# Sign words on GpSimd, dummy transposes at the start, and two new tables of places in an attention and two-layer kernel

## The chip, the cores and the metric

One core of one Trainium2 chip. The metric is the device time of one execution in microseconds; the kernel before takes 914.72 us (median of three runs, 914.27 to 915.67).

## The reference

Three stages follow each other. Attention with rotated q and k, four batches of eight heads, 576 positions, 64 columns a head; then a gated layer on 2304 tokens; then a second layer with a softmax-weighted activation and a normalisation.

```python
q_rot, k_rot = (rotate(q), rotate(k))
scores = scale * np.matmul(q_rot, k_rot.transpose(0, 1, 3, 2))
attn = np.exp(scores - np.max(scores, axis=-1, keepdims=True))
attn = attn / (np.sum(attn, axis=-1, keepdims=True) + 1e-09)
x = np.matmul(attn, v)                       # then laid out as 2304 x 512
gate = 1.0 / (1.0 + np.exp(-(x @ w_gate)))   # 512 x 1536
x = gate * (x @ w_val) @ w_out               # 1536 x 512
h = x @ w_in                                 # 512 x 1024
solu = h * softmax(h)
ln = (solu - mean) / np.sqrt(var + 1e-06) * g_ln
out = ln @ w_out2                            # 1024 x 512
```

The weights of the layers come as 64-bit floats. The kernel reads them as pairs of 32-bit words and makes 32-bit floats of them itself.

## The kernel before, in words

**Two-term products.** Every 32-bit operand is split into a high part, as the matmul takes it, and a low part (the rest): ScalarE or VectorE copies the high part, VectorE or GpSimd subtracts. A product is three matmuls (high x high, high x low, low x high) or, in attention, stacked so that two do.

**Attention** works on 16 pairs of heads, nine tiles a pair (four for each head and one for the 64 left positions of both). For each pair q and k are loaded and rotated on GpSimd (lines 162 and 170; the first pair is rotated mostly on VectorE, lines 186 and 170), transposed on TensorE (the banks, lines 222 and 225), split into stacks (370 and 373; for pair 0 lines 249, 251 and 256), and some blocks are copied by DMA (line 238). A tile is then: scores on TensorE (291), row maximum on VectorE (298), exponential on ScalarE (303), transposes of the result on TensorE (379), their split on ScalarE (370) and VectorE (373), and the products with v (420). Scores alternate between two PSUM buffers, so the scores of tile n+2 wait for the exponential of tile n. The results are added (431) and scaled (351) on GpSimd.

The order of all of that is not found while the kernel is built. Every job has a name such as `scores.4.0@0` (its tile, step and pair) and a number in the table NEED, to which 16.83 times the pair is added. `emit_attention` sorts the jobs by that number into one queue for each engine; each queue is then issued strictly in that order. The other figures of an attention job (its cost `took`, its gate, its port) are not read by it.

**The first pair** is prepared ahead of the table: loads, rotation, and the transposes of three banks (0 is k, 1 is q, 2 is the left positions of both). `stack_first(h, step, m)` then evacuates them for head h: step 0 the 512 main positions, step 1 the 64 left ones, with m 0 and 1 the high parts of k and q on ScalarE, m 2 and 3 the low parts on VectorE, and step 2 copies k's block to the other half. In the table these are `first.h.step.m`.

**The gated layer** runs three groups of weights s over three blocks of tokens b of 768 each. Each block has four units (two gates, two values) of 42 or 48 matmul rows on seven products of quarters, and two output halves. Weights are made ahead of their use by `decode`: a load of raw words; the magnitude on ScalarE (463); the sign word (466), an OR with the magnitude (469) and an OR with the low word (474) on VectorE. Then come sums (483) and splits (486, 494). `make_pair` does two decodes for each of four units from s=1 on, `make_plain` two in all, `make_unit` one for each of twelve output weights, `keep_p` eight and `keep_i` eight for the last stage: 46 decodes. Six more weights are decoded during attention by `job_early`, which calls the same three steps. Tokens are split into xs by `split_x` (535, 540, 544). In the output halves results leave PSUM on ScalarE or VectorE (486) and go to memory, from s=1 on by DMAs of GpSimd's queue that add (1457).

**The planner of these stages** is `run_jobs`. Each job has an engine or a choice of two, a cost, what it reads and writes, and a due time `need`. On each engine, of the jobs that are ready first, the one due first is taken; TensorE's own order is fixed. Jobs marked with a port are kept from running on VectorE and GpSimd together.

**The last stage** computes the hidden layer, the normalisation and the second product by tiles of 128 tokens in the same planner.

The lines the change and the prediction touch: `qk_bank` (212 to 228), `w_sign` (465), the block after `table` (651 to 671), `job_scores` (723), the NEED table (1027), `decode` (1204), `KEEP_I` (1316), and `run_jobs` (1721).

Of the kernel before, what the change touches and what calls it, by code (L numbers as in the profile page):

```python
# [20 lines left out]
def kernel(  # L21
# [21 lines left out]
    nc = tc.nc  # L43
# [605 lines left out]
    if True:  # L649
# [72 lines left out]

    def job_scores(g):
# [7 lines left out]
        took = (1.06 if order[n] is None else 0.53) * (2.0 if g < 4 else 1.0)  # L731
        writes = [one(f"S{g % 2}")] + ([one(f"sum{i % 4}", 0, NTL)] if n == 0 else [])
        ajob(nc.tensor, took, lambda: found.__setitem__(("s", g), scores(i, n)), reads, writes)
# [8 lines left out]
    def turned_out(took, fn, reads, hi_at, lo_at, cols):  # L742
        t, key = bank_t(), ("t", turns[0])
        ajob(nc.tensor, took, lambda: found.__setitem__(key, fn()), reads, (t,))
        ajob(A, 0.045 + cols / 1190, lambda: [evac_h(*ev) for ev in found[key]], (t,), hi_at)
        ajob(V, 0.07 + cols / 960, lambda: [evac_l(*ev) for ev in found.pop(key)], [t] + hi_at, lo_at)

    def job_te(i, n):
# [3 lines left out]
        turned_out(0.436 * (2.0 if i * NTL + n < 2 else 1.0), lambda: transpose_e(i, n), [one(f"e{(i * NTL + n) % 7}", 0, 1)], hi_at, lo_at, 512)  # L752

    def job_corner(i):
        hi_at, lo_at = ([one(f"etl{h}{a}", MAIN, S) for h in range(2)] for a in range(2))
        turned_out(0.03, lambda: transpose_corner(i), [one(f"e{(i * NTL + 4) % 7}", 1, 2)], hi_at, lo_at, 128)
# [10 lines left out]
    def job_attend(i, h, j, m0, m1):  # L767
# [4 lines left out]
        if m1 == 9:  # L772
            e = (A, V)[SLOTS["uw"][2 * h + j]]
            ajob(e, 0.365 if e is V else 0.3, lambda: high(e, *found["av"][0][1:]), (one("AV"),), (one(uw, *c),))
# [21 lines left out]
    def job_weigh_out(i):  # L796
        ajob(V, 0.2, lambda: weigh_out(i, 0), (found.pop(("tr", i)),), (one("rt"),))
# [35 lines left out]
    def job_split_v(i):  # L833
        raw, hi, lo = one(f"rawv{i % 2}", 0, 3), one(f"vs{i % 2}", 0, 1), one(f"vs{i % 2}", 1, 2)
        ajob(A, 0.63, lambda: split_v(i, 0), (raw,), (hi, lo, one("order_vs")))
# [124 lines left out]
    for m, t in enumerate((7.9, 10.0, 10.25)):  # L960
# [60 lines left out]
    for m in chunks:  # L1021
# [939 lines left out]
```

## Time and profile before

| what | value |
|---|---|
| median of three runs | 914.72 us |
| profiled execution, its own time | 915.11 us |
| its span, first to last instruction | 913.2 us |
| mean granted clock of TensorE | 0.997 |
| busy: TensorE, VectorE, ScalarE, GpSimd | 882.9, 810.2, 653.5, 339.3 us |

The span is what the rows below divide; 1.9 us of the execution's time lie outside it. Attention fills the span to about 290 us, the gated layer from there to about 705, the last stage the rest. TensorE's matmuls are pipelined, so a row's length is that of one matmul from its start to its last result, and the next begins before.

### The profile page before, as it was taken

The numbers are of one execution on the slowest core, as the hardware profiler recorded it, in microseconds if no ns is written. First come the engines' busy times: TensorE is split into PE (matmuls) and PEld (weight loads), VectorE is DVE, ScalarE is ACT, GpSimd is POOL, SyncE is SP. The second block draws the span as 40 slices with busy tenths as digits, with TensorE's granted clock in tenths as the row PEclk, the third lists the DMA queues.
The fourth block names the chain that finished last, engine by engine and source line by source line (L and its number), as shares of the span: only waits on it lengthen the run. The fifth ranks groups of instructions, "written<-read, shape, count | busy, mean of one in ns | idle before, by whom it ended". The sixth has DMA issues, their size and how long they took to land.

```text
span 913.2 us, 16106 instructions
## 1 busy us (share of the span) xinstructions
PE 882.9 (97%) x5354; PEld 833.1 (91%) x5354; DVE 810.2 (89%) x1523; ACT 653.5 (72%) x1379; POOL 339.3 (37%) x296
## 2 busy tenths in 40 slices
PE   4999999999999999999999999999999999999998
PEld 3999999999998999999999999999999877888886
DVE  5999999999997798999998999999987499999971
ACT  4999999999995465666667666666565276777751
POOL 7679899898845000011011121212030243233200
PEclk9999999999999999999999999999999999999999
DMA  4667777678663762425275864659599834454332
GB/s 127 159 183 196 205 200 197 184 209 214 155 165 112 221 216 81 151 81 196 86 230 135 260 133 145 129 174 229 179 250 364 185 124 93 99 109 81 81 70 46
DMA packets 120882, 147.33 MB, mean 161 GB/s; under 512 B 44752, under 2 KB 90080, under 8 KB 120800
## 3 DMA queue, kind: packets, MB, share of 16 engines
q1 hardware_dynamic: 113888, 136.87, 51.4%
q0 software_dynamic: 6912, 9.44, 7.1%
q8 instruction: 42, 0.69, 0.3%
q14 instruction: 40, 0.33, 0.1%
HBM read 77.76 MB, written 37.30 MB: 126 GB/s over the span
## 4 chain that ended last, share of the span: by engine, by line
PE 73%; DVE 19%; issue 3%; DMA 2%; ACT 2%; POOL 0%; SPq 0%; DVEq 0%; ACTq 0%
PE s L291 9%; PE av L420 8%; PE te L379 7%; DVE xs L544 2%; PE tq L222 2%; PE far_c L1869 2%; PE far_b L1869 2%; PE far_c L1871 2%; PE far_b L1870 2%; PE far_c L1870 2%; PE far_b L1871 2%; PE tk L400 1%; DVE w L469 1%; PE near_a L630 1%; PE near_a L629 1%
## 5 line engine op out<-in xcount | busy, mean ns | idle before, releaser
L298 DVE TENSOR_REDUCE nm<-s 128x1 f32<-128x576 f32 x144 | 108.2, 752 | 11.5 <-PE s L291 9.0
L303 ACT ACTIVATE e<-s,nm 128x576 f32<-128x576 f32 x144 | 107.7, 748 | 7.4 <-DVE nm L298 6.0
L291 PE MATMUL s<-st 128*128 128x288 f32 x512 | 96.6, 312 | 5.5 <-DVE st L251 3.9
L373 DVE TENSOR_TENSOR et<-te,et 128x512 fp32r<-128x512 f32 x144 | 95.8, 676 | 1.4 <-ACT et L370 1.3
L420 PE MATMUL av<-et,vs 128*128 128x288 f32 x512 | 94.4, 312 | 0.4 <-POOL vs L202 0.4
L1457 POOL DMA_DIRECT2D yd<-yst x40 | 36.0, 1280 | 141.1 <-ACT yst L486 141.1
L370 ACT CAST et<-te 128x512 fp32r<-128x512 f32 x144 | 81.2, 587 | 7.8 <-PE te L379 6.4
L379 PE MATMUL te<-ident,e 128*128 128x128 f32 x576 | 81.9, 274 | 2.5 <-DVE et L373 2.4
L291 PEld LDWEIGHTS s<-st 128*128 128x128 f32 x512 | 75.1, 193 | 6.8 <-ACT st L249 4.2
L420 PEld LDWEIGHTS av<-et,vs 128*128 128x128 f32 x512 | 73.3, 191 | 0.7 <-POOL vs L202 0.6
L379 PEld LDWEIGHTS te<-ident,e 128*128 128x128 f32 x576 | 67.4, 141 | 5.1 <-DVE et L373 2.5
L540 ACT CAST xs<-xst 128x384 fp32r<-128x384 f32 x110 | 50.7, 518 | 13.7 <-DVE xst L535 11.5
L544 DVE TENSOR_TENSOR xs<-xst,xs 128x384 fp32r<-128x384 f32 x112 | 56.4, 548 | 2.2 <-ACT xs L540 2.0
L1538 POOL TENSOR_TENSOR xs<-xst,xs 128x512 fp32r<-128x512 f32 (+1 forms) x14 | 17.5, 1254 | 72.7 <-ACT xs L1535 72.7
L431 POOL TENSOR_TENSOR x_sb<-uw,um 64x576 f32<-64x576 f32 x30 | 43.2, 1439 | 2.5 <-DMA um<-uw 0.4
L494 POOL TENSOR_TENSOR wv<-w,wv 128x512 fp32r<-128x512 f32 (+1 forms) x3 | 5.2, 1743 | 103.3 <-ACT wv L486 103.3
L170 POOL TENSOR_TENSOR turned_t<-raw_t,other_t 128x576 f32<-128x576 f32 (+1 forms) x30 | 40.5, 1369 | 1.2
L463 ACT ACTIVATE mag<-raw_w 128x512 f32<-128x512 f32 x52 | 34.9, 676 | 7.9 <-DMA raw_w<-in_moe_w_val_dram 3.7
L162 POOL TENSOR_TENSOR other_t<-raw_t,rope_sb 128x1152 f32<-128x1152 f32 x14 | 37.4, 2674 | 5.6 <-DMA raw_t<-in_q_dram 4.5
L162 POOL TENSOR_TENSOR raw_t<-raw_t,rope_sb 128x1152 f32<-128x1152 f32 x14 | 37.3, 2664 | 1.1
L1811 POOL TENSOR_TENSOR st<-st,mhalf 128x1 f32<-128x1 f32 x18 | 15.9, 884 | 54.9 <-DVE st L1810 53.7
L629 PE MATMUL near_a<-xs,wg 128*128 128x384 f32 x96 | 32.3, 337 | 2.1 <-ACT held L1363 2.1
(475 smaller groups left out, 3068.4 us busy)
## 6 DMA issues: line engine op xcount, KB each, us to landing
st<-st SPq DMA_DIRECT2D x45, 288.0 KB, 4.0
xst<-xd SPq DMA_DIRECT2D x32, 384.0 KB, 6.0
raw_w<-in_moe_w_out_dram SPq DMA_DIRECT2D x20, 512.0 KB, 4.5
yd<-yst POOLq DMA_DIRECT2D x40, 192.0 KB, 6.5
st<-st SPq DMA_DIRECT2D x47, 144.0 KB, 2.4
raw_w<-in_moe_w_gate_dram SPq DMA_DIRECT2D x12, 512.0 KB, 4.3
raw_w<-in_moe_w_val_dram SPq DMA_DIRECT2D x12, 512.0 KB, 3.7
cd<-mag SPq DMA_DIRECT2D x22, 256.0 KB, 5.5
```

The lines of the kernel that those rows point to most:

```text
L162: eng.tensor_mul(out=(o, x)[step], in0=x, in1=w.to_broadcast([P, n, 2, D // 2]))
L291: nc.tensor.matmul(ps[:, j, :HALF], w, x, start=m == 0, stop=m == len(mm) - 1)
L298: nc.vector.tensor_reduce(out=nm, in_=ps[:, :, :HALF], axis=AX.XY, op=ALU.max, negate=True)
L303: nc.scalar.activation(out=e.rearrange("p (j c) -> p j c", j=2), in_=ps[:, :, :HALF], func=AF.Exp, bias=nm, accum_out=sums[i][:, n:n + 1],)
L370: nc.scalar.copy(out=h_out, in_=ps)
L373: nc.vector.tensor_sub(out=l_out, in0=ps, in1=h_out.bitcast(F32))
L379: nc.tensor.transpose(ps[:, r * P:(r + 1) * P], e[:, r * P:(r + 1) * P], ident)
L420: nc.tensor.matmul(av[:, :HALF], *mm[m], start=m == 0, stop=m == len(mm) - 1)
L431: eng.tensor_add(out=x_sb[hp][rows, b * S:(b + 1) * S], in0=uws.pop((i, h))[rows], in1=uws[i][rows])
L540: nc.scalar.copy(out=t[:, 0], in_=here)
L544: l_eng.tensor_sub(out=t[:, 1], in0=here, in1=t[:, 0].bitcast(F32))
L629: nc.tensor.matmul(out, wh, t[:, 0], start=fresh and j == 0, stop=False, skip_group_check=not fresh)
```

## The change

1. **Sign words.** `decode` no longer masks the sign on VectorE. GpSimd multiplies the upper raw word, taken as a float, by zero, which leaves a zero with that sign. `job_early` keeps the mask on VectorE.
2. **Dummies.** Transposes of the identity into a PSUM tile of the attention products that is not read: 30 before the three banks of pair 0, 16 behind them, and 5, 5 and 4 behind the scores of tiles 1, 2 and 3 of pair 0.
3. **Tables.** All but three of NEED's 446 numbers are new. A second table, SHIFT, with 945 entries, is added to the due times of the jobs of the later stages, which get names for that.
4. **Others.** `qk_bank` sets the stacks at every part, since part 2 may now be first; costs and gates of attention jobs are changed; the second layer's first weights are prepared 6 and 5 us earlier in their blocks.

```diff
     def qk_bank(i, part):
-        if part == 0:
-            stacks[i, 0] = st_t[i % 2][0]
-            stacks[i, 1] = st_t[i % 2][1]
+        stacks[i, 0], stacks[i, 1] = st_t[i % 2]
...
+    def w_zero(raw, dst):
+        nc.gpsimd.tensor_scalar(out=dst.bitcast(F32), in0=words(raw)[1].bitcast(F32), scalar1=0.0, scalar2=None, op0=ALU.mult)
...
+        idle_ps = ps_av.tile([P, 512], F32, tag="av", name="idle")
+
+        def keep_clock(n):
+            for _ in range(n):
+                nc.tensor.transpose(idle_ps[:, 0:P], ident, ident)
+
+        keep_clock(30)
         first.extend(qk_bank(0, part)[0][2] for part in range(3))
-        pass
+        keep_clock(16)
...
+    IDLE_AFTER = {1: 5, 2: 5, 3: 4}
...
-        took = (1.06 if order[n] is None else 0.53) * (2.0 if g < 4 else 1.0)
+        took = 1.06 if order[n] is None else 0.53
+        if i == 0 and n in IDLE_AFTER:
+            took += 0.11 * IDLE_AFTER[n]
...
+        def run():
+            found["s", g] = scores(i, n)
+            if i == 0 and n in IDLE_AFTER:
+                keep_clock(IDLE_AFTER[n])
...
     NEED = {
...
-        "early_split.1.0.1": 315.64, "early_split.1.1.0": 293.71, "early_split.1.1.1": 316.34, "first.0.0.0": -33.81,
-        "first.0.0.1": -62.21, "first.0.0.2": -32.31, "first.0.0.3": -12.85, "first.0.1.0": -47.13, "first.0.1.1": -19.51,
-        "first.0.1.2": -23.78, "first.0.1.3": -7.03, "first.0.2.0": -23.49, "first.0.2.1": -19.51, "first.1.0.0": -47.43,
-        "first.1.0.1": -21.09, "first.1.0.2": -39.4, "first.1.0.3": -6.96, "first.1.1.0": -21.89, "first.1.1.1": -14.81,
-        "first.1.1.2": -8.4, "first.1.1.3": -5.83, "first.1.2.0": -34.61, "first.1.2.1": 1.45, "join.0.0": 34.59,
...
+        "early_split.1.0.1": 329.84, "early_split.1.1.0": 307.9, "early_split.1.1.1": 321.54, "first.0.0.0": -155.18,
+        "first.0.0.1": -148.61, "first.0.0.2": -124.38, "first.0.0.3": -91.43, "first.0.1.0": -90.42, "first.0.1.1": -149.16,
+        "first.0.1.2": -100.02, "first.0.1.3": -104.32, "first.0.2.0": -67.98, "first.0.2.1": -41.76, "first.1.0.0": -71.56,
+        "first.1.0.1": -41.22, "first.1.0.2": -84.48, "first.1.0.3": -21.85, "first.1.1.0": -30.56, "first.1.1.1": -2.47,
+        "first.1.1.2": -66.08, "first.1.1.3": -14.93, "first.1.2.0": -101.44, "first.1.2.1": -74.49, "join.0.0": 35.91,
...
+    plain_job, names_of = job, []
+    SHIFT = {
+        "unit.1.2.0.17": -14, "unit.1.2.0.18": 0.8, "unit.1.2.0.3": -3.9, "unit.1.2.0.4": 17.4, "unit.1.2.0.8": -2.5,
...
+        "x.2.0.28": 14.4, "x.2.0.3": 7.5, "x.2.0.30": 12, "x.2.0.33": -4.9, "x.2.0.34": -0.6, "x.2.0.35": 5.4,
...
+    }
+    def place(*name):
+        step[:] = [".".join(map(str, name)), None, 0]
+
+    def job(eng, took, fn, reads=(), writes=(), need=0.0, port=None):
+        key = f"{step[0]}.{step[2]}"
+        step[2] += 1
+        names_of.append(key)
+        plain_job(eng, took, fn, reads, writes, need + SHIFT.get(key, 0.0), port)
...
     def decode(kind, n, dst, dst_at, need):
...
-        job(V, 0.34, lambda: w_sign(raw, dst), (r,), (dst_at,), need - 5, True)
+        job(G, 0.9, lambda: w_zero(raw, dst), (r,), (dst_at,), need - 5, False)
...
-    KEEP_I = {(2, 0): (0, 36.0), (2, 1): (1, 25.0)}
+    KEEP_I = {(2, 0): (0, 30.0), (2, 1): (1, 20.0)}
```

## Rows read from the trace of the kernel before

**Rows 1.** The page: busy time of each engine, and TensorE's granted clock in 40 slices.

```profile
PE 882.9 (97%) x5354; PEld 833.1 (91%) x5354; DVE 810.2 (89%) x1523; ACT 653.5 (72%) x1379; POOL 339.3 (37%) x296
PEclk9999999999999999999999999999999999999999
```

**Rows 2.** Stretches: length, then busy us (instructions) of each engine, granted clock, DMA.

```profile
100.00:150.00 50.00, 50.00 (x398) 48.02 (x397) 48.66 (x85) 47.41 (x114) 44.74 (x34) 1.00 0.75 196
290.00:700.00 410.00, 404.12 (x2310) 400.47 (x2309) 377.14 (x739) 263.31 (x560) 50.31 (x52) 1.00 0.60 178
310.00:340.00 30.00, 28.00 (x155) 26.47 (x155) 27.79 (x54) 18.39 (x38) 0.74 (x1) 1.00 0.74 252
340.00:400.00 60.00, 60.00 (x348) 60.00 (x347) 54.55 (x112) 37.76 (x83) 0.00 (x0) 1.00 0.32 110
400.00:450.00 50.00, 49.41 (x284) 48.77 (x283) 48.80 (x98) 33.32 (x71) 6.52 (x4) 1.00 0.40 137
550.00:600.00 50.00, 47.78 (x264) 46.98 (x263) 49.03 (x95) 31.46 (x67) 9.70 (x10) 0.97 0.53 129
580.00:585.00 5.00, 5.00 (x22) 5.00 (x21) 4.83 (x11) 2.51 (x5) 2.14 (x3) 0.66 1.08 147
600.00:650.00 50.00, 49.47 (x285) 49.15 (x285) 48.43 (x95) 33.46 (x72) 8.51 (x9) 1.00 0.72 207
```

**Rows 3.** Timeline around 577 us: start, length, engine, line, what it does.

```profile
577.16 1.48 DVE L544 TENSOR_TENSOR xs<-xst,xs 128x384 fp32r<-128x384 f32 x3
...
579.06 0.44 PE L629 MATMUL near_a<-xs,wg 128*128 128x384 f32 x1 [1.96 <-ACT held L1363]
```

**Rows 4.** Timeline from the start to 16 us.

```profile
1.00 0.29 POOL masks.py:199 TENSOR_SCALAR_AFFINE_SELECT ident<-ident 128x128 f32<-128x128 f32 x1
...
6.89 1.09 PE L222 MATMUL tq<-ident,turned_t 128*128 128x128 f32 x4 [6.89 <-DVE turned_t L170]
...
9.90 0.44 PE L225 MATMUL tq<-ident,turned_t 128*128 128x128 f32 x1
...
10.14 1.40 ACT L249 CAST st<-tq 64x512 fp32r<-64x512 f32 x3 [4.61 <-PE tq L222]
...
12.69 0.67 ACT L256 CAST st<-st 64x576 fp32r<-64x576 f32 x1
...
14.24 0.58 PE L291 MATMUL s<-st 128*128 128x288 f32 x1 [3.90 <-DVE st L251]
```

**Rows 5.** Timeline from 15 to 32 us.

```profile
15.42 2.76 POOL L170 TENSOR_TENSOR turned_t<-w,other_t 128x576 f32<-128x576 f32 x2
...
16.81 0.76 DVE L298 TENSOR_REDUCE nm<-s 128x1 f32<-128x576 f32 x1 [0.90 <-PE s L291]
...
23.20 1.68 PE L291 MATMUL s<-st,qtl 128*128 128x288 f32 x8
...
25.48 2.79 POOL L170 TENSOR_TENSOR turned_t<-raw_t,other_t 128x576 f32<-128x576 f32 x2
...
31.11 0.60 PE L222 MATMUL tq<-ident,turned_t 128*128 128x128 f32 x4
```

**Rows 6.** VectorE's groups from 290 to 700 us: count, busy us, mean ns.

```profile
L544 DVE TENSOR_TENSOR xs<-xst,xs 128x384 fp32r<-128x384 f32 x112 | 56.4, 548 | 2.2 <-ACT xs L540 2.0
...
L474 DVE SCALAR_TENSOR_TENSOR w<-raw_w,w 128x512 int32<-128x512 int32 x28 | 19.3, 689 | 0.7
...
L466 DVE TENSOR_SCALAR w<-raw_w 128x512 int32<-128x512 int32 x28 | 12.6, 453 | 4.3 <-DMA raw_w<-in_moe_w_gate_dram 2.5 <-DMA raw_w<-in_moe_w_val_dram 1.5
...
L1261 DVE TENSOR_TENSOR rawv<-w,mag 128x512 fp32r<-128x512 f32 x14 | 9.4, 682 | 0.0
```

**Rows 7.** GpSimd's groups by shape: the two-input operation on 512 columns.

```profile
L494 POOL TENSOR_TENSOR wg<-w,wg 128x512 fp32r<-128x512 f32 x4 | 5.1, 1285 | 18.6 <-ACT wg L486 18.6
```

**Rows 8.** Timelines of GpSimd and VectorE at 127.6 us.

```profile
127.60 0.23 POOL L263 CAST qtl<-st 128x64 fp32r<-128x64 f32 x1
...
127.61 0.77 DVE L474 SCALAR_TENSOR_TENSOR w<-raw_w,w 128x512 int32<-128x512 int32 x1
```

More of the change, by code (lines that the diff above doesn't have):

```diff
@@ L730, in job_scores @@
             reads.append(one(f"qtl{i % 2}", 0, 2))
-        took = (1.06 if order[n] is None else 0.53) * (2.0 if g < 4 else 1.0)
+        took = 1.06 if order[n] is None else 0.53
+        if i == 0 and n in IDLE_AFTER:
+            took += 0.11 * IDLE_AFTER[n]
         writes = [one(f"S{g % 2}")] + ([one(f"sum{i % 4}", 0, NTL)] if n == 0 else [])
-        ajob(nc.tensor, took, lambda: found.__setitem__(("s", g), scores(i, n)), reads, writes)
+        def run():
+            found["s", g] = scores(i, n)
+            if i == 0 and n in IDLE_AFTER:
+                keep_clock(IDLE_AFTER[n])
+        ajob(nc.tensor, took, run, reads, writes)
     def job_softmax(g):
@@ L773, in job_attend @@
             e = (A, V)[SLOTS["uw"][2 * h + j]]
-            ajob(e, 0.365 if e is V else 0.3, lambda: high(e, *found["av"][0][1:]), (one("AV"),), (one(uw, *c),))
+            ajob(e, 0.365 if e is V else 0.39, lambda: high(e, *found["av"][0][1:]), (one("AV"),), (one(uw, *c),))
     def job_join(i, h):
@@ L796, in job_weigh_out @@
     def job_weigh_out(i):
-        ajob(V, 0.2, lambda: weigh_out(i, 0), (found.pop(("tr", i)),), (one("rt"),))
+        ajob(V, 0.27, lambda: weigh_out(i, 0), (found.pop(("tr", i)),), (one("rt"),))
         ajob(SP, 0.2, lambda: weigh_out(i, 1), (one("rt"),), (one(f"d{i % 2}"),))
@@ L834, in job_split_v @@
         raw, hi, lo = one(f"rawv{i % 2}", 0, 3), one(f"vs{i % 2}", 0, 1), one(f"vs{i % 2}", 1, 2)
+        if i == 0:
+            gate[len(jobs)] = 10.8
         ajob(A, 0.63, lambda: split_v(i, 0), (raw,), (hi, lo, one("order_vs")))
@@ L851, in job_stack_left @@
         for h in range(2):
-            ajob(G, 0.2, lambda h=h: stack_left(i, h), row_stacks(i, h, 1, 2, "l"), (one(f"qtl{i % 2}", h, h + 1),))
+            ajob(G, 0.25, lambda h=h: stack_left(i, h), row_stacks(i, h, 1, 2, "l"), (one(f"qtl{i % 2}", h, h + 1),))
     first_t = []
@@ L959 @@
     begin("turned", None)
-    for m, t in enumerate((7.9, 10.0, 10.25)):
+    for m, t in enumerate((7.5, 9.7, 9.85)):
         gate[len(jobs)] = t
@@ L1230, in make_pair @@
     def make_pair(s, n, need):
+        place("pair", s, n)
         for j in range(2):
@@ L1238, in make_plain @@
     def make_plain(n, need):
+        place("plain", n)
         of, done = 1024 * (n % 2), (2, 2, 2, 0)[n]
@@ L1250, in make_again @@
     def make_again(n, need):
+        place("again", n)
         job(SP, 1.7, lambda: nc.sync.dma_start(out=w32[:, 0:1024], in_=wd[n]), (one(f"wd{n}"),), (one("w32", 0, 1024),), need - 12)
@@ L1265, in keep_p @@
     def keep_p(n, need):
+        place("keep", n)
         k = raws_used[0] % 2
@@ L1278, in keep_i @@
     def keep_i(c, need):
+        place("keep_i", c)
         quarter = {f"B{m + 1}{n + 1}": slice(1024 * m + 512 * n, 1024 * m + 512 * n + 512) for m in range(2) for n in range(2)}
@@ L1304, in load_unit @@
     def load_unit(c, need):
+        place("cd", c)
         at_ = C_AT[c]
@@ L1315 @@
     KEEP = {(1, 1): range(0, 5), (1, 2): range(5, 8)}
-    KEEP_I = {(2, 0): (0, 36.0), (2, 1): (1, 25.0)}
+    KEEP_I = {(2, 0): (0, 30.0), (2, 1): (1, 20.0)}
     def make_unit(kind, n, where, need):
+        place("w", kind, n)
         k = raws_used[0] % 2
@@ L1328, in load_x @@
     def load_x(b, need):
+        place("x", *now, b)
         for kk in range(KD):
@@ L1352, in unit @@
     def unit(s, b, n_unit, done=0):
+        place("unit", s, b, n_unit)
         q, kind, setn = n_unit // 2, "gv"[n_unit % 2], n_unit % 2
@@ L1425, in output @@
     def output(s, b, half, setn):
+        place("out", s, b, half)
         bank, need = banks[setn], out_at(s, b, half)
@@ L1463 @@
     END = unit_at(*LAST, 4) + 2 * OUT
+    now = [0]
     for s in range(NF // FG):
+        now[:] = [s]
         if s:
@@ L1525, in job_y @@
     def job_y(p_, need):
+        place("y", p_)
         st = lambda lo, n=1: one("xst", 1024 * (p_ % 2) + 256 * lo, 1024 * (p_ % 2) + 256 * (lo + n))
@@ L1581, in job_h @@
     def job_h(p_, need):
+        place("h", p_)
         names = set_names(p_)
@@ L1633, in job_n @@
     def job_n(t, need):
+        place("n", t)
         ph_at, scr = [e_at(t)], one(f"scr{t % 2}")
@@ L1650, in job_p @@
     def job_p(t, need):
+        place("p", t)
         pk, tp = pk_at(t), one(f"tp{t % NTP}")
@@ L1657, in job_u @@
     def job_u(t, need):
+        place("u", t)
         tp = one(f"tp{t % NTP}")
@@ L1669, in job_turn_ln @@
         hi_w, lo_w = LT_AT[t % 2]
+        had = list(step)
+        place("turn", t)
         for n in range(2):
@@ L1675, in job_turn_ln @@
             job(V, 0.6, lambda n=n: turned_ln(t, n, 1), (at_, hi), (lo,), need + n + 1, False)
+        step[:] = had
     def job_j(t, need):
+        place("j", t)
         at_ = one("bank", 5 + t % 2, 6 + t % 2)
@@ L1703 @@
             names += [f"sg{q_}{x}" for q_ in range(2) for x in "abcd"] + ["held1", "held5", "heldu", "held4"]
+            place("open")
             job(V, 0.01, lambda: open_pools(), (), [one(n, 0, 2) for n in names] + [one("xs4", 0, 4 * HT), one("X")], END + 2, False)
```

8 lines of the change are left out of this document (4 added, 4 removed), and 325 rows, old and new, of tables (NEED, SHIFT).

## The prediction

> **What bounds the kernel now.** The page comes first: in a span of 913.2 us TensorE is busy 882.9 and VectorE 810.2 [rows 1]. The busy share of a pipelined TensorE hides short gaps, so I next cut the span into stretches and counted matmuls [rows 2]. From 340 to 400 us 348 matmuls of 384 columns take 60.00 us, 0.1724 us each: that is the pace when nothing is late. At that pace the same table shows what is lost: 155 where 174 fit (310 to 340), and 284, 264 and 285 for 290 (from 400, 550 and 600). The deficits are 19, 6, 26 and 5, together 56 matmuls or 9.7 us (an estimate: a few records can be missing). Attention in the middle has TensorE at 50.00 of 50 with VectorE at 48.66: both are full, and an order alone can win little there.
>
> The largest deficit, 26 matmuls or 4.5 us, I followed in the timeline [rows 3]. TensorE stands still for 1.96 us, until 579.06. The row names a copy on ScalarE, but VectorE is in the middle of a run of xs subtractions without a pause (577.16), and the next product reads those xs: VectorE is late. Then the clock is lost as well: after that pause the granted clock of 580 to 585 is 0.66 of full, part of it at the 1.2 GHz level, and 22 matmuls run where 29 fit, 1.2 us more [rows 2].
>
> Last the start, by its timeline [rows 4, 5]. The first turned bank takes 1.09 us for four transposes; at 31.11 four take 0.60. The granted clock is in its top tenth in every slice of the span [rows 1], but the pace of the first is near half. ScalarE sits until 10.14 for its first evacuation, because its queue begins with q, the second bank. The first score is at 14.24, the first row maximum at 16.81.
>
> **Part 1: the attention tables and the dummies.** The attention jobs are put in order by their place numbers alone. The edited costs and gates of that stage (scores, turned-out, weigh, split v) are not read there, so they cost and bring nothing. The order matters, and the two tables, sorted, give the head of each queue. ScalarE took q of head 0, k of head 1, the short rest, then k of head 0. It will take k of head 0 first (its bank ends at 6.89+1.09=7.98), then the rest of q, q, the rest of k, k of head 1, then both far copies.
>
> After the last bank (about 10.1) ScalarE has two short ones (an eighth of the columns, some 0.2 each by estimate), two of 0.47 (1.40 for three [rows 4]) and two far copies of 0.60 (0.67 busy, overlapping): 2.56 us, so 12.7, and the first score about 12.75 with all it needs. VectorE's subtractions fit beside that. The first maximum comes near 13.5 instead of 16.81, 3.3 us sooner.
>
> The dummies: 30 transposes start when the identity is there, at 1.29 [rows 4]. At the slow pace (1.09 for four and 0.44 for one, so 0.65 for three more, 0.22 each) they take at most 6.6 us and end by 7.9, against a first real transpose at 6.89. So they delay bank 0 by 1.0 at most and nothing else waits for it but one ScalarE copy that has until 10.1. If the pace doubles halfway they delay nothing. The 16 behind the turned q lie between 10.2 and 12.7, where TensorE waits anyhow (3.90 us before 14.24). The 5, 5 and 4 behind scores 1, 2 and 3 are 14 x 0.11 = 1.5 us in places where TensorE waits for exponentials. If that cover is gone they cost 1.5.
>
> What is late next is GpSimd: pair 1 is rotated at 15.42+2.76=18.18 as before [rows 5], and its banks stand ahead of score 4 in TensorE's queue. At the doubled pace they take 1.0, so score 4 runs at about 19.2 instead of 23.20, 4.0 gained. Pair 2 is rotated at 25.48+2.79=28.27, unmoved; its banks were turned at 31.11 and would now be asked for at 27.1, so 1.2 of it is given back. I take **-3.0 us**; bounds -4.4 (nothing given back) and -1.0 (only the pace of the first score rows gained).
>
> For the rest of attention I take 0, since no instruction goes away: SP, GpSimd and VectorE issue what they did, in a new order. Bounds -3 and +3.
>
> **Part 2: sign words.** 46 of the 48 sign words between 290 and 700 move (the decodes of this stage; the early weights keep theirs). On VectorE one is 0.453 in the mean [rows 6], so 46 x 0.45 = 20.8 us leave it, of 377.1 busy in that stretch [rows 2]. On GpSimd, busy 50.3 of 410, they have room. The row for its length is missing. Nearest are a GpSimd operation with one input on 128 columns, 0.29 [rows 4], and one with two inputs on 512, 1.285 [rows 7]. The new one has one input and four times the columns; I take 0.65, nearer the first, ends 0.29 and 1.29.
>
> It waits for the raw words and for its place in w32 or a value buffer. Behind it in GpSimd's queue are the accumulating yd writes and some low halves; they wait for nothing late, and six yst buffers cover one word. The two OR steps now wait for another engine; the magnitude on ScalarE runs beside it, so a decode grows by 0.2 at most, hidden while weights are made ahead.
>
> What is not free is that GpSimd holds VectorE. At 127.60 a GpSimd cast of 0.23 runs, and the OR step that starts beside it takes 0.77 [rows 8] for 0.689 in the mean [rows 6]: it ends with the cast plus 0.55, so a hold is the rest of the GpSimd operation less 0.13. Casts with one input hold too. Ten groups of VectorE with two inputs from SBUF, 56.4 (L544) down to 9.4 (L1261) [rows 6], sum to 212 of 377 us: 56%. So by estimate a word holds VectorE 0.56 x (0.65-0.13) = 0.29 us, and the net is 0.45-0.29=0.16 each, 7.4 us over the stage. Ends: no hold, 20.8 relieved; every word held at 1.29, 46 x (1.16-0.45) = 33 us added.
>
> The page GPSIMD Engine Reference of the Trainium skill (§ 1, Specifications) speaks against this edit: GpSimd shares its SBUF interfaces with VectorE and collides with any two-input operation. By that alone, if each word met such work, a word would cost 0.52 for 0.45 saved and the stage 46 x 0.07 = 3 us of VectorE instead of winning 7.4. The cast of [rows 8] agrees that one input is enough to hold; the 56% speak for the smaller price.
>
> **Part 3: the table of shifts** (945 entries) and the earlier second weights (30 for 36, 20 for 25 us behind the block's start) remove no instruction. They change which of the waiting jobs VectorE, ScalarE, GpSimd and SP take first, and thereby every place where VectorE is late. Against the 9.7 us of deficits: the stop at 577 (4.5 with its clock) has the words of four weight pairs ahead of it in VectorE's queue and I let 3.4 of it go; of the other 5.2 I let half go and take 1.0 of that back for new stops. Sum **-5.0 us**; bounds -10 (all of it) and +8 (below). The last stage: 0.
>
> **Sum.** 915.11 (span 913.2 and 1.9 around it) - 3.0 - 5.0 = 907.1. That execution is 0.4 above the median of the three runs, 914.72, so 906.7; I say 907.
>
> **Rivals.** *The shifts take all stops away.* The deficits are 9.7 us and VectorE has 410-377=33 us free in the stage, so it is possible; against it, a stop moves more often than it goes. 915.1-4.4-9.7=901, and 898 if the last stage gives 3 as well; I take 899; chance 0.13. *Only the start comes.* The holds (0.29) eat the relief and the new order makes as many stops as it removes: 915-3=912; chance 0.18. *Slower: the words hold VectorE.* If a word lasts 0.9 us and lands mostly among runs of two-input work (as at 577.16, three in a row), the hold is 0.8 x 0.77=0.62 against 0.45 saved, 46 x 0.17=8 us more on VectorE at the moments when weights are made and xs are split, which is where TensorE already waits. Worked as stops of TensorE: +8, with the start -3: 920. It decides from a mean hold of 0.45 on. For it: the held OR step [rows 8]; against it: GpSimd's words can run in the 44% of other work. Chance 0.12. That page's rule is this rival. *Nothing seen*: gains and losses cancel, or the clock falls again before 24 us: 914.7; chance 0.05. The forecast has 0.52.
>
> **How the numbers follow.** A change under 0.2% (1.8 us) can't be told from none here. Faster: 0.52+0.13 and most of the third, 0.77. Same: 0.10. Slower: 0.13. The range goes from the first rival to just past no change, 899 to 915; what is left out is most of the slower case and a tail of the best one.
>
> **What would show it.** In the changed profile: first maximum near 13.5, score 4 near 19.2, pair 2's banks at 28.3; four transposes near 0.6 us from 9 us on; 46 GpSimd operations of 0.65 us; OR steps above 0.69 beside them; 285 matmuls or more in the 50 us behind the 573.8 start, and the granted clock 1.00 there. The forecast is wrong if the first maximum stays above 15.5, if the words last over 0.9, or if the middle stage loses more than 56 matmuls in these four stretches.

## The result, and the profile after

The changed kernel takes 923.72 us (median of four runs, 921.87 to 924.71) where the kernel before takes 914.5 beside it: ratio 1.0096 [1.0075, 1.0117], 9 us slower. The forecast was 907. The profiled execution took 922.83 us, its span is 921.0.

The page of the changed kernel: busy time of the engines, and the granted clock in 40 slices.

```profile
PE 893.4 (97%) x5414; PEld 842.9 (92%) x5414; DVE 797.4 (87%) x1482; ACT 661.1 (72%) x1383; POOL 416.5 (45%) x333
PEclk9999999999999899999999999999999999999999
```

Against [rows 1] VectorE has 12.8 us less to do and GpSimd 77.2 more. Most of TensorE's extra 10.5 us are the dummies. One slice of the clock, the fourteenth (299 to 322 us), is below its top tenth.

The stretches of the changed kernel, columns as in [rows 2].

```profile
300.00:305.00 5.00, 0.62 (x2) 0.30 (x2) 2.61 (x5) 2.71 (x5) 0.00 (x0) 0.73 0.40 136
305.00:310.00 5.00, 4.76 (x17) 4.77 (x18) 2.15 (x5) 1.62 (x3) 1.18 (x1) 0.58 0.96 286
310.00:340.00 30.00, 26.14 (x138) 25.15 (x137) 26.15 (x47) 15.58 (x32) 9.56 (x6) 0.94 0.72 240
340.00:400.00 60.00, 59.67 (x345) 59.35 (x344) 51.27 (x103) 36.52 (x80) 6.53 (x4) 1.00 0.30 104
400.00:450.00 50.00, 48.86 (x276) 47.31 (x275) 49.18 (x92) 33.38 (x70) 21.37 (x10) 1.00 0.39 131
550.00:600.00 50.00, 47.39 (x261) 46.26 (x260) 48.52 (x90) 33.13 (x70) 20.44 (x16) 0.97 0.54 136
600.00:650.00 50.00, 50.00 (x291) 50.00 (x290) 47.23 (x89) 32.44 (x72) 18.27 (x15) 1.00 0.69 192
290.00:700.00 410.00, 395.95 (x2220) 390.15 (x2220) 358.64 (x673) 257.82 (x545) 126.97 (x92) 0.98 0.59 174
```

Two matmuls run between 300 and 305 us. From 310 to 340 there are 138 where 155 ran before; 400 to 450 and 550 to 600 lose too, only 600 to 650 is full. GpSimd's load rose from 50.3 to 127.0, more than twice what 46 words of 0.65 would add.

The start of the changed kernel, its timeline.

```profile
1.35 5.44 PE L674 MATMUL idle<-ident 128*128 128x128 f32 x30 [1.35 <-POOL ident masks.py:199]
6.92 0.65 PE L220 MATMUL tq<-ident,turned_t 128*128 128x128 f32 x4
14.02 1.42 DVE L296 TENSOR_REDUCE nm<-s 128x1 f32<-128x576 f32 x2
19.39 1.32 PE L289 MATMUL s<-st,qtl 128*128 128x288 f32 x8
28.54 0.66 PE L220 MATMUL tq<-ident,turned_t 128*128 128x128 f32 x4 [1.39 <-POOL turned_t L170]
```

Here all went nearly as forecast: the first bank takes 0.65 us instead of 1.09 [rows 4], the first maximum comes at 14.02 (forecast 13.5) instead of 16.81, score 4 at 19.39 instead of 23.20, and pair 2's banks wait for GpSimd [rows 5]. The dummies and the new order of the first pair were never run apart, so what each of them gave is not shown.

The end of attention in the changed kernel, timelines of SP, VectorE and TensorE.

```profile
295.10 0.29 SPq L331 DMA_DIRECT2D d<-rt  x1
296.36 0.72 SPq L424 DMA_DIRECT2D um<-uw  x1
293.19 0.43 DVE L464 TENSOR_SCALAR w<-raw_w 128x512 int32<-128x512 int32 x1 [2.99 <-DMA raw_w<-in_moe_w_gate_dram]
294.81 0.27 DVE L327 COPY rt<-tr 9x128 f32<-9x128 f32 x1
299.64 0.76 DVE L429 TENSOR_TENSOR x_sb<-uw,um 64x576 f32<-64x576 f32 x1 [3.97 <-DMA um<-uw]
302.76 0.76 DVE L349 TENSOR_TENSOR x_sb<-x_sb,wt 128x576 f32<-128x576 f32 x1 [2.36 <-DMA wt<-d]
301.63 0.44 PE L644 MATMUL near_b<-xs,wg 128*128 128x384 f32 x1 [1.72 <-ACT sg L1579]
305.24 0.69 PE L646 MATMUL near_b<-xs,wg 128*128 128x384 f32 x1 [2.99 <-DVE wg L495]
```

TensorE stands 1.72 and 2.99 us here. VectorE waits 2.99 us for the raw words of an early weight, with the copy of rt behind that step, and then 3.97 and 2.36 us for DMAs of the last pair. The same milestones (start in us) show where the time went; "new attention" and "two places" are runs e3 and e13 below.

| | before | after | new attention (e3) | two places (e13) |
|---|---|---|---|---|
| first score of pair 1 | 33.73 | 30.18 | 30.02 | 30.03 |
| first score of pair 15 | 264.50 | 260.56 | 262.14 | 259.87 |
| end of the last product with v | 296.43 | 290.51 | 292.07 | 289.83 |
| first output product | 323.89 | 324.82 | 325.66 | 318.44 |
| second output half | 334.04 | 338.11 | 335.41 | 329.00 |
| first product of the hidden layer | 715.77 | 724.66 | 717.12 | 710.74 |
| end of the span | 913.19 | 921.04 | 914.57 | 908.18 |

Attention ends 5.9 us earlier. By the first output product that is lost and 0.9 more, by the second half 4.1 are lost, by the hidden layer 8.9; the last stage gives 1 back. (The changed kernel and e3 have the same attention order; at pair 15 single executions differ by 1.6 us.)

GpSimd's words and the OR steps that wait for them, groups of the changed kernel from 290 us on.

```profile
L467 POOL TENSOR_SCALAR w<-raw_w 128x512 f32<-128x512 f32 x26 | 43.6, 1684 | 130.3 <-DVE w L484 35.5 <-DVE wg L495 28.2 <-DMA raw_w<-in_moe_w_val_dram 28.1
L467 POOL TENSOR_SCALAR rawv<-raw_w 128x512 f32<-128x512 f32 x20 | 41.0, 2058 | 67.0 <-DMA raw_w<-in_moe_w_out_dram 36.8 <-DMA cd<-rawv 20.5 <-DVE far_b L1567 8.2
L470 DVE SCALAR_TENSOR_TENSOR w<-mag,w 128x512 int32<-128x512 int32 x27 | 20.1, 745 | 7.6 <-POOL w L467 6.8 <-ACT mag L461 0.7
L470 DVE SCALAR_TENSOR_TENSOR rawv<-mag,rawv 128x512 int32<-128x512 int32 x20 | 14.1, 706 | 2.9 <-POOL rawv L467 2.8
```

A word lasts 1.68 and 2.06 us in the mean, not 0.65, and VectorE stands 9.6 us in front of OR steps whose word is not there.

### The profile page after: what moved, and what is told of

Same layout as the page of the kernel before. It is cut to its first block, busy times and chain, and to the rows that moved or that the text cites. A ratio compares the mean times of both kernels' runs of the same rounds, so it can differ in the third digit from the quotient of the medians.

```text
span 921.0 us, 16349 instructions
## 1 busy us (share of the span) xinstructions
PE 893.4 (97%) x5414; PEld 842.9 (92%) x5414; DVE 797.4 (87%) x1482; ACT 661.1 (72%) x1383; POOL 416.5 (45%) x333
## 4 chain that ended last, share of the span: by engine, by line
PE 73%; DVE 13%; DMA 5%; POOL 3%; issue 2%; ACT 2%; SPq 1%; POOLq 0%; DVEq 0%; ACTq 0%
PE s L289 7%; PE av L418 7%; PE te L377 5%; DVE xs L545 2%; PE far_c L2083 2%; PE far_c L2081 2%; PE far_b L2081 2%; PE far_c L2082 2%; PE far_b L2083 2%; PE far_b L2082 2%; PE far_a L630 2%; PE near_a L631 2%; PE far_a L631 2%; PE far_a L632 2%; PE near_a L630 2%
## 5 line engine op out<-in xcount | busy, mean ns | idle before, releaser
L467 POOL TENSOR_SCALAR w<-raw_w 128x512 f32<-128x512 f32 x26 | 43.6, 1684 | 130.3 <-DVE w L484 35.5
L289 PE MATMUL s<-st 128*128 128x288 f32 x512 | 98.8, 314 | 0.8 <-ACT st L254 0.6
L377 PE MATMUL te<-ident,e 128*128 128x128 f32 x576 | 86.4, 273 | 1.2 <-ACT e L301 0.9
L368 ACT CAST et<-te 128x512 fp32r<-128x512 f32 x144 | 83.8, 585 | 4.4 <-PE te L377 3.4
L289 PEld LDWEIGHTS s<-st 128*128 128x128 f32 x512 | 72.4, 190 | 2.0 <-ACT st L254 0.8
L467 POOL TENSOR_SCALAR rawv<-raw_w 128x512 f32<-128x512 f32 x20 | 41.0, 2058 | 67.0 <-DMA raw_w<-in_moe_w_out_dram 36.8
L545 DVE TENSOR_TENSOR xs<-xst,xs 128x384 fp32r<-128x384 f32 x112 | 61.9, 591 | 0.7 <-ACT xs L541 0.4
L1741 POOL TENSOR_TENSOR xs<-xst,xs 128x512 fp32r<-128x512 f32 (+1 forms) x16 | 20.2, 1272 | 67.9 <-ACT xs L1738 42.3
```

What stands on the lines that cost most here:

```text
L289: nc.tensor.matmul(ps[:, j, :HALF], w, x, start=m == 0, stop=m == len(mm) - 1)
L368: nc.scalar.copy(out=h_out, in_=ps)
L377: nc.tensor.transpose(ps[:, r * P:(r + 1) * P], e[:, r * P:(r + 1) * P], ident)
L467: nc.gpsimd.tensor_scalar(out=dst.bitcast(F32), in0=words(raw)[1].bitcast(F32), scalar1=0.0, scalar2=None, op0=ALU.mult)
L545: l_eng.tensor_sub(out=t[:, 1], in0=here, in1=t[:, 0].bitcast(F32))
```

## The experiments

Theories: **T1**, the words cost the time, because the chain of a decode gets longer (T1a) or because GpSimd and VectorE hold each other (T1b); **T2**, the table of shifts does; **T3**, the new places at the end of attention do. Ratios are to runs of the kernel before, taken beside each run.

**e1, e2: one part undone.** In e1 `job(G, 0.9, w_zero)` is `job(V, 0.34, w_sign)` again; in e2 the shifts are left out.

```diff
-        plain_job(eng, took, fn, reads, writes, need + SHIFT.get(key, 0.0), port)
+        plain_job(eng, took, fn, reads, writes, need, port)
```

> The changed kernel with one part undone: decode masks the sign on VectorE again; the two tables, the dummies and the rest of the change stay. T1 (the words on GpSimd, 1.53 us and more each, make the weights late and hold VectorE, and cost the 9 us): 909 to 912 us, and the stop near 302 us goes. T2 (the table of shifts puts jobs of the gated layer at worse places): 921 to 924. T3 (the new places at the end of attention make the first weights of the gated layer late, 290 to 340 us): 919 to 923, with the stops at 299.6 and 301.9 us still there.

> The changed kernel with another part undone: the table of shifts is not added to the due times; the words stay on GpSimd and the attention table stays new. T1: 921 to 928 (the words still cost what they cost). T2: 910 to 914. T3: 919 to 923 with the stops between 299 and 303 us still there, since the shifts do not reach the attention jobs.

Measured: e1 935.86, 1.0230 [1.0215, 1.0245]; e2 929.47, 1.0162 [1.0147, 1.0177]. T2 falls: the shifts gain 5.75 us. But they gain them only with the words on GpSimd: with the words on VectorE the same table makes the kernel 12 us slower than the changed one. The table seems to fit one plan only, so e1, outside all three forecasts, says nothing on T1.

**e3, e4: one part alone**, on the kernel before: the new attention table with the dummies (e3); the words on GpSimd (e4).

> One part alone on the kernel before: the new attention table with the dummies; sign words on VectorE, no shifts, the second layer's first weights at their old times. T1 and T2: 909 to 911 (the 4 to 6 us that the attention gains by its last product stay, nothing is lost behind it). T3: 915 to 919, the block behind attention starting 1 to 4 us later than in the kernel before, as in the changed one.

> One part alone on the kernel before: decode makes the sign word on GpSimd; old attention table, no dummies, no shifts. T1: 920 to 928, GpSimd busy some 127 us between 290 and 700 as in the changed kernel. T2 and T3: 913 to 917, since VectorE gets 20.8 us of sign words off and some 13 us of holds on.

Measured: e3 916.47, 1.0018 [1.0008, 1.0028]; e4 930.13, 1.0163 [1.0146, 1.0179]. T1 and T3 both hold. In steps from the kernel before to the changed one: new attention +1.5 (e3), words with the earlier second weights +13.0 (e2 less e3), shifts -5.75 (changed kernel less e2). These three end at 923.7 by construction; what tests them is e4, where the words alone cost 15.2 us. In e4, 3 us are lost by the second output half and 6.8 in the first 50 us of the last stage.

**e5: the new places for the first pair alone**, everything else of the old table.

> The kernel before with the dummies and with the new table's places for the first pair alone (the names of the first pair, of its stacks, and of the banks of the second); every other place, those of the end of attention among them, is the old one. The gated layer is the old one. T3 (in the run with the whole new table the 4.4 us that attention had gained by its last product were lost between 290 and 326 us because the new places put the last pair's chain of weights, the copy of rt, the stores of d and wt and the scaling of x_sb, later against the last product, and VectorE and ScalarE stand behind them): 910 to 911.5, last product near 292, first output product near 320. Rival (what follows attention is not set by TensorE there, and any earlier end of attention is waited off): 913.5 to 915, first output product near 324.

Measured: 920.42, 1.0048 [1.0032, 1.0063], a miss of both: the two tables seem not to fit together, and 4.1 us gained at pair 1 have become 2.4 lost at pair 2. It does not decide T3; that attention's end 2.23 late makes the first output product 2.25 late shows only that lateness is passed on.

**e6, e7, e8: which words, which order.** In e6 only the weight pairs and the eight kept weights take the new word; e7 is e4 with `job(G, 1.6, ..., True)`, the longer cost and the port mark; e8 keeps `w_sign` and adds `w_zero` into a tile that nothing reads.

> The kernel before with GpSimd's sign words in 24 of the 46 decodes: the weight pairs of the second and third group and the eight kept weights, which are made ahead of their use; the 22 others (first group, output weights, first weights of the second layer) mask the sign on VectorE. T1a (a word costs because it stands in a chain of load, word, two OR steps and splits that is walked just before its use): 913 to 918, and neither the 3.1 us between 324 and 337 nor the 6.8 us between 721 and 751 of the run with all 46 words come back. T1b (a word costs because it and VectorE hold each other): 24 of 46 of 15 us, so 921 to 924.

> The kernel before with all 46 sign words on GpSimd, and the planner told what they measure: cost 1.6 instead of 0.9, and marked as keeping VectorE's marked work away. If the loss of the run with 46 words comes from an order made with a wrong cost: 915 to 920. If it comes from the chain itself (T1a), which no order shortens: 927 to 933, the same as without.

> The kernel before with the sign word on VectorE as it was, and beside it the same GpSimd operation into a tile that nothing reads, 46 times. It keeps the holds between GpSimd and VectorE and takes the chain and the relief of VectorE away. T1a (chain): 914 to 918. T1b (holds): 921 or more.

Measured: e6 916.91, 1.0011 [1.0000, 1.0022]; e7 966.73, 1.0553 [1.0529, 1.0576]; e8 926.60, 1.0117 [1.0097, 1.0137]. In the planner's order the 24 words ahead of their use cost next to nothing in sum. That seems to put the harm on the 22 made just in time, but e10 below does not bear it out. e8 shows that a word costs without anybody waiting for it. In e7, outside both forecasts, the planner, told the true cost, made a worse order (one stop of 13.07 us at 349 us, before an output weight), so planned costs do not heal it. In all of these the planner also moves other jobs; in the next pair it does not.

**e10, e11: the same with every other instruction where it was before.** The planner keeps counting a VectorE step of 0.34; in e11 VectorE also keeps its own word.

```diff
-        job(V, 0.34, lambda: w_sign(raw, dst), (r,), (dst_at,), need - 5, True)
+        job(V, 0.34, lambda: w_zero(raw, dst), (r,), (dst_at,), need - 5, True)
```

> The kernel before with all 46 sign words on GpSimd, but the planner still counts each as the VectorE step that it was (0.34), so that every other instruction of every engine stands in the order of the kernel before. T1a/T1b (chain and holds, which are there in any order): 922 to 931. If the loss of the run with 46 words is the planner's new order alone: 911 to 916, since VectorE has 20.8 us less to do.

> The kernel before, all orders as they were, with the GpSimd operation on the raw words into a tile that nothing reads beside each sign word, which stays on VectorE. Only the holds and the later release of a raw buffer are left. If the 11 us of the earlier run with words that nobody waits for were the planner's new order: 914.5 to 917. If they were holds: 921 or more.

Measured: e10 922.35, 1.0081 [1.0061, 1.0101]; e11 926.59, 1.0123 [1.0107, 1.0140]. So the words cost 7.4 us with every order kept. That is half of e4's 15.2: e4 and e10 differ in the planner's order alone, and it costs the other 7.8. From 290 us to the end, busy times of e11, where nobody waits, and of the kernel before in the same stretch (columns as in [rows 2]):

```profile
290.00:925.60 635.60, 615.15 (x3259) 576.09 (x3257) 555.04 (x1059) 393.29 (x759) 180.29 (x155) 0.99 0.53 151
```

```profile
290.00:913.20 623.20, 610.05 (x3258) 572.86 (x3256) 543.94 (x1060) 394.01 (x761) 104.73 (x109) 1.00 0.55 154
```

The same VectorE instructions take 11.1 us more beside 46 words, 0.24 each: the hold. The time is 11.3 longer by the ratio, and VectorE's idle time in the stretch is almost the same (80.6 and 79.3 us), so what the hold adds to VectorE comes out at the end. (A raw buffer is also released later in e11; the two were not tried apart, but VectorE's waits for raw words before its own sign words grow only from 4.3 to 5.1 us.) The same stretch of e10:

```profile
290.00:921.90 631.90, 613.60 (x3263) 574.03 (x3261) 536.20 (x1014) 393.57 (x762) 180.67 (x155) 1.00 0.54 152
```

The groups of its words and of its first OR step, last the idle time before it and what ended that:

```profile
L467 POOL TENSOR_SCALAR w<-raw_w 128x512 f32<-128x512 f32 x26 | 45.1, 1740 | 132.1 <-DVE w L484 52.7 <-DVE wg L495 28.7 <-DMA raw_w<-in_moe_w_val_dram 21.2
L467 POOL TENSOR_SCALAR rawv<-raw_w 128x512 f32<-128x512 f32 x20 | 35.0, 1752 | 55.3 <-DMA raw_w<-in_moe_w_out_dram 30.9 <-DMA cd<-rawv 18.6 <-DVE wo L1520 5.8
L470 DVE SCALAR_TENSOR_TENSOR w<-mag,w 128x512 int32<-128x512 int32 x28 | 20.7, 740 | 14.2 <-POOL w L467 11.0 <-ACT mag L461 3.1
L470 DVE SCALAR_TENSOR_TENSOR rawv<-mag,rawv 128x512 int32<-128x512 int32 x20 | 15.2, 761 | 5.7 <-POOL rawv L467 5.1 <-ACT mag L461 0.5
```

VectorE has 7.7 us less to do, as forecast (7.4), but the OR steps wait 11.0 + 5.1 = 16.1 us for their words, and VectorE's queue with them. One such wait, in timelines of GpSimd and VectorE, and another on VectorE:

```profile
396.00 1.52 POOL L467 TENSOR_SCALAR w<-raw_w 128x512 f32<-128x512 f32 x1 [23.44 <-DVE wg L495]
397.56 0.69 DVE L470 SCALAR_TENSOR_TENSOR w<-mag,w 128x512 int32<-128x512 int32 x1 [1.64 <-POOL w L467]
494.73 0.69 DVE L470 SCALAR_TENSOR_TENSOR rawv<-mag,rawv 128x512 int32<-128x512 int32 x1 [1.64 <-POOL rawv L467]
```

The word starts as soon as its place is free and lasts 1.52 us, and VectorE stands through all of it. Both of these weights are made ahead of their use, a pair's and a kept one. Read one by one in the trace, there are 12 such waits, and 8.9 of the 16 us stand in front of the 24 weights made ahead: the step behind the word stands in an in-order queue, and what comes behind it there is needed sooner.

**e14, e15: is it the length?** Old order in both. e14 makes the word on ScalarE, `activation(..., scale=0.0)`, which leaves a zero without a sign, so the signs of these weights are left out. In e15 GpSimd makes 128 columns, and puts them into two small tiles of their own instead of the weight's place.

```diff
-        nc.gpsimd.tensor_scalar(out=dst.bitcast(F32), in0=words(raw)[1].bitcast(F32), ...)
+        nc.gpsimd.tensor_scalar(out=dst.bitcast(F32), in0=words(raw)[1].bitcast(F32)[:, 0:128], ...)
```

> The kernel before with the 46 sign words of decode made on ScalarE (a copy with scale 0), all other instructions in the order of the kernel before. VectorE is relieved by 20.8 us as with GpSimd, the word comes from a third engine too, but ScalarE is not one that held VectorE in any row here. If the relief was eaten by the holds and by the long word: 906 to 912. If a word from another engine costs by itself, or VectorE's relief is worth nothing: 914 to 920.

> As the run with 46 GpSimd words in the old order, but a word is made of 128 of its 512 columns, and the first OR step uses these signs for all four quarters (the signs of the other three are left out). The word should last 0.4 to 0.5 us. If the length of the word is the matter (1.54 us in the median, the OR step behind it waiting and VectorE held meanwhile): 906 to 912. If a hand-over to GpSimd costs at any length: 918 to 922.

Measured: e14 913.43, 0.9981 [0.9971, 0.9991], between its two forecasts; e15 909.45, 0.9939 [0.9924, 0.9954]. The groups of e15:

```profile
L467 POOL TENSOR_SCALAR scrap<-raw_w 128x128 f32<-128x128 f32 x46 | 34.5, 750 | 191.8 <-DMA raw_w<-in_moe_w_out_dram 45.9 <-DVE w L489 37.3 <-DMA raw_w<-in_moe_w_in_dram 32.6
L475 DVE SCALAR_TENSOR_TENSOR w<-mag,scrap 128x512 int32<-128x512 int32 x26 | 17.8, 686 | 4.6 <-ACT mag L461 3.1 <-POOL scrap L467 1.2
L475 DVE SCALAR_TENSOR_TENSOR rawv<-mag,scrap 128x512 int32<-128x512 int32 x20 | 15.1, 756 | 2.8 <-ACT mag L461 1.6 <-POOL scrap L467 0.7 <-ACT held_u L1566 0.4
```

Two stretches of e15:

```profile
290.00:909.10 619.10, 609.05 (x3263) 572.23 (x3261) 529.59 (x1014) 394.28 (x762) 135.42 (x155) 1.00 0.55 155
550.00:600.00 50.00, 49.48 (x283) 48.48 (x282) 48.86 (x92) 33.16 (x72) 14.86 (x17) 1.00 0.56 142
```

The groups of e14:

```profile
L470 DVE SCALAR_TENSOR_TENSOR w<-mag,w 128x512 int32<-128x512 int32 x28 | 20.0, 714 | 10.7 <-ACT w L467 7.2 <-ACT mag L461 3.2
L470 DVE SCALAR_TENSOR_TENSOR rawv<-mag,rawv 128x512 int32<-128x512 int32 x20 | 14.4, 718 | 6.8 <-ACT rawv L467 5.7 <-ACT mag L461 1.2
```

The stretch from 290 us of e14:

```profile
290.00:913.80 623.80, 610.19 (x3263) 572.44 (x3262) 530.45 (x1014) 417.37 (x808) 104.43 (x109) 1.00 0.55 154
```

Words of 0.75 us cost 1.9 us of waiting, and the stop at 577 us is gone: 283 matmuls between 550 and 600, where [rows 2] has 264. ScalarE's words hold nobody, but stand behind the magnitude on the same engine and make VectorE wait 12.9. The four old-order runs in one table, VectorE's busy time against before plus its wait for words:

| run (one profiled execution) | busy | wait for the word | sum | time by the ratio |
|---|---|---|---|---|
| e11, read by nobody | +11.1 | 0 | +11.1 | +11.3 |
| e10, GpSimd, 512 columns | -7.7 | 16.1 | +8.4 | +7.4 |
| e14, ScalarE | -13.5 | 12.9 | -0.6 | -1.7 |
| e15, GpSimd, 128 columns | -14.4 | 1.9 | -12.5 | -5.6 |

Order and sign agree. A part of the waits only changed its place, since VectorE used to wait for raw words before its own sign words; with the growth of all waits before the steps of a decode (2.0, 14.4, 12.0 and 4.9 us) the sums are +13.1, +6.7, -1.5 and -9.5, nearer the times in all but e11. So what decides is the wait: e14's words, 0.67 us each, are as short as e15's, yet they make VectorE wait 12.9 us. e15 differs from e10 in two things, though, the length and the place: its words need not wait until the weight's place is free. By estimate length alone takes at most some 10 us of the 14.2 between them, since each of e10's 12 waits can get shorter by no more than 1.52 less 0.53 us; length and place were not tried apart. Why VectorE's gain in e15 is not all gained in time is not shown.

**e9, e12, e13: the end of attention.** VectorE takes the copy of rt behind the sign word and first OR step of the sixth early weight, which wait for raw words; SP stands in front of `d<-rt` meanwhile, with `um` and `wt` behind it. e9 (on e3) and e12 (on the changed kernel) move that one number to 67; e13 (on e3, the edit below) moves it to a better place, and the last part of `wt` too.

```diff
-        "weigh_out.0@15": 88.3,
+        "weigh_out.0@15": 77,
-        "spread.1@15": 118.07,
+        "spread.1@15": 73.2,
```

> The kernel before with the whole new attention table and the dummies (as in the third run), and one number of that table changed: the place of the last pair's copy of rt on VectorE, weigh_out.0@15, from 88.3 to 67. There it no longer stands behind the OR steps of the last early weight, which wait for its raw words, and SP's queue, which waits with the store of d, is released some 8 us sooner. T3: 910 to 911.5, the copy of rt near 288.5, the stops at 301 and 304 us gone. If the loss between 290 and 326 us has another cause than this copy: 915 to 917 as in the third run.

> The changed kernel with the same one number changed (the copy of rt at 67 instead of 88.3), everything else of the change kept. T3 and T1 together: the 4 to 5 us that the end of attention lost come back and the words' cost stays, 918 to 920. If what follows is late for the words anyway: 922 to 924.

> The kernel before with the whole new attention table and the dummies, and two numbers of that table changed: the copy of rt (weigh_out.0@15) at 77, so that it stands behind the OR steps of the fifth early weight and ahead of those that wait for the sixth one's raw words (at 67 it waited 1.6 us for TensorE and the sixth load left 1.2 us later), and the last part of wt (spread.1@15) at 73.2, ahead of three stores of x on SP. If the end of attention is set by the load of the sixth weight and by the scaling behind wt: 911 to 912.5, the stop near 301.7 us (2.5) down to about 1. If by something else: 913.5 to 914.5, as with the copy at 67.

Measured: e9 914.03, 0.9990 [0.9980, 1.0000], 2.4 less than e3 and between its two forecasts; e12 919.42, 1.0051 [1.0036, 1.0066], 4.3 less than the changed kernel; e13 911.18, 0.9957 [0.9943, 0.9970], 5.3 less than e3. T3 is shown. The timelines of e13 at the end of attention:

```profile
289.46 0.38 SPq L331 DMA_DIRECT2D d<-rt  x1
288.84 0.27 DVE L327 COPY rt<-tr 9x128 f32<-9x128 f32 x1
297.55 0.76 DVE L349 TENSOR_TENSOR x_sb<-x_sb,wt 128x576 f32<-128x576 f32 x1 [1.40 <-DMA wt<-d]
300.03 0.45 PE L646 MATMUL near_b<-xs,wg 128*128 128x384 f32 x1 [0.45 <-DVE wg L495]
```

Against the changed kernel the copy runs at 288.84 instead of 294.81, the scaling at 297.55 instead of 302.76, and stops of 4.7 us become one of 0.45. (e3, from which e13 differs in these two numbers alone, has the copy at 296.49, the scaling at 304.28 and stops of 1.84 and 2.83.) e13 is faster than both kernels: the new attention order and the dummies kept, two places mended, sign words and shifts left away.

**e16, e17, e18: words on top of e13.** e16 takes ScalarE's words without a sign; e17 and e18 read the magnitude instead of the raw words, on ScalarE and on GpSimd. The order puts some words of e17 and e18 ahead of their magnitude, so they take the sign of an earlier one, and in e18 the next magnitude waits for GpSimd.

> The two numbers of the thirteenth run and the words on ScalarE of the fourteenth together, orders otherwise as they were. If the two add up: 2.5 to 3.5 less than the better of the two alone. If ScalarE's words make the weights at the end of attention later: no better than the thirteenth run.

> As the sixteenth run, but ScalarE makes the word from the magnitude, which still has the sign, by a scale of 2 to the minus 100 that leaves a zero; the copy with scale 0 in the fourteenth and sixteenth runs left a zero without a sign. The time should be that of the sixteenth, 908 to 910: the word is as long and stands behind the magnitude on the same engine as before.

> The two numbers of the thirteenth run, and the words on GpSimd in the old order, made from the magnitude, whose words lie side by side, instead of every second word of the raw tile. If the stride makes the word 1.54 us long: 0.7 to 1.0 us a word and 908 to 911. If 512 columns take 1.5 us on GpSimd at any stride: the cost of the tenth run on top of the thirteenth, and the word starts later behind the magnitude, 918 to 922.

Measured: e16 908.69, 0.9937 [0.9921, 0.9953]; e17 910.52, 0.9940 [0.9922, 0.9957]; e18 934.28, 1.0198 [1.0181, 1.0215]. None of the three makes all signs, so e13 stays the fastest that does; e16 fits the two gains adding up (-3.9 and -1.7 us by the ratios, -5.8 together), though its interval overlaps e13's. The time of e18, outside both forecasts, mixes two causes, but the length of its words can be read, one of GpSimd's two groups:

```profile
L467 POOL TENSOR_SCALAR w<-mag 128x512 f32<-128x512 f32 x26 | 42.3, 1628 | 152.5 <-ACT mag L461 56.8 <-DVE w L484 51.5 <-DVE wg L495 26.1
```

Side by side (1.63 us here, 1.88 for the 20 others) or at a stride of two (1.74 in e10), 512 columns take about as long: the stride is not it.

## Why the prediction was wrong, point by point

**The start** (-3.0): right, nearly step by step; 3.5 us at pair 1's first score. The dummies hid behind the wait for the first bank, and the bank ran at the fast pace.

**The rest of attention** ("I take 0, since no instruction goes away"): this step failed. I had sorted the two tables and read the heads of the queues, not the tails. One copy that the new order leaves behind a wait for raw words costs 4.3 us in the changed kernel (e12), and the whole of attention costs 1.5 instead of giving 3.0; so the rest took 4.5, beyond the bound of 3.

**The sign words** (-7.4 us of VectorE, and no term of their own in the sum): the main failure, in two terms. The length, taken as 0.65 with 1.29 as the upper end, is 1.74 in the mean of e10. The two-input row of [rows 7] was no bound for a one-input operation. And "a decode grows by 0.2 at most, hidden while weights are made ahead" is wrong twice: the OR steps wait 16.1 us, and being made ahead hides little of it, since 8.9 of them stand before weights made ahead. In place of nothing the words cost 7.4 us in the old order (e10), and 13.0 in the changed kernel's before the shifts, the earlier second weights with them.

Two forecasts here came true by luck: the hold, 0.29 by estimate and 0.24 measured, and the net on VectorE, 7.4 forecast and 7.7 measured. The estimate was for a word of 0.65 us. By its own formula, 0.56 x (length - 0.13), taken from one row [rows 8], a word of 1.74 holds VectorE 0.90 us; e11 shows about a quarter of that. So the formula was wrong too, and its error hid that of the length. With a word of 0.75 us and a place of its own the stop at 577 is gone and e15 is 5.6 us faster, the way the forecast had it.

**The slower rival** had the sign and nearly the time (920), but not the mechanism: it needed a mean hold of 0.45, and the hold is 0.24. The wait for the word took its place, a cost that I had priced at nothing. The rule behind it (the Trainium skill, GPSIMD Engine Reference, § 1 Specifications: interfaces shared with VectorE's two-input operations) agrees with e11, where nothing but the hold and the kept raw buffer is added and 11.1 us go.

**The shifts** (-5.0): -5.75 measured, near the forecast by luck and not for the reason given. The stop at 577, which I let go, stays (2.00 us at 585 in the changed kernel). Between e2 and the changed kernel 5.5 us of the difference arise from 742 to 773 us, early in the last stage, which I had set to 0. The shifts help only with the words on GpSimd, and they give back about what the planner's order costs there (7.8 by e4 and e10); that they mend this order is a reading and not shown. The earlier second weights went with the shifts in e1 and with the words in e2; they were not tried alone.

**What was to show it**: two of the three signs against the forecast came true. Words last over 0.9, and the four stretches run 138 + 276 + 261 + 291 = 966 of 174 + 3 x 290 = 1044, 78 lost where 56 were. The first maximum was in time.

## What to carry to other kernels

When a step moves to another engine, price the wait of the step behind it and not only the work saved: the same relief of some 20 us was worth -5.6 with a word of 0.75 us in a place of its own and +7.4 with one of 1.74. That a product is made ahead does not hide the wait: ask what else stands in the in-order queue behind the step that takes it. In an order written as a table, look for the in-order queues behind each wait: two numbers of 446 were worth 5.3 us.

## What the runs showed of the hardware that was not expected

**A one-input operation on GpSimd is not cheap.** With VectorE idle beside it a word of 128 columns takes 0.53 us (e15, below) and one of 512 takes 1.52 (e10 at 396.00, above), about 2.6 ns a column by that difference. The Trainium skill (GPSIMD Engine Reference, § 4.1 Engine selection) calls one-input operations roughly line rate; the measurement decides.

```profile
539.49 0.53 POOL L467 TENSOR_SCALAR scrap<-raw_w 128x128 f32<-128x128 f32 x1 [7.20 <-DMA raw_w<-in_moe_w_val_dram]
```

**The word can lose too.** In the changed kernel, VectorE goes on with two-input operations while two words take 9.20 us, the first of them 7.35. Timelines of GpSimd and VectorE:

```profile
432.80 9.20 POOL L467 TENSOR_SCALAR rawv<-raw_w 128x512 f32<-128x512 f32 x2 [8.52 <-DMA raw_w<-in_moe_w_out_dram]
434.93 1.49 DVE L545 TENSOR_TENSOR xs<-xst,xs 128x384 fp32r<-128x384 f32 x3
436.81 1.49 DVE L545 TENSOR_TENSOR xs<-xst,xs 128x384 fp32r<-128x384 f32 x3
```

Three subtractions take 1.49 us here, against 1.48 in [rows 3], so VectorE is not slowed: this time GpSimd is the one that is held.

**The clock after a pause.** In e13 a pause of 1.99 us, before 574.04, is followed by a granted clock of 0.66 from 575 to 580, part of it at the lower level of 1.2 GHz. In the changed kernel two short ones (0.82 and 0.55 us, by 681.03) are followed by 0.66 too, while in e4 one of 2.86 us, before 757.30, is followed by 1.00. The length of a pause alone does not tell.

**A zero's sign.** GpSimd's product with zero keeps it (e10). ScalarE's copy with scale zero loses it, as far as e14 shows, whose weights differ from e10's by that instruction alone.
